# A cross-network kernel on one core: whole-tile transposes of the first input group, and the last round's outputs transposed on TensorE

## The chip, the cores and the metric

The kernel runs on 1 core of one Trainium2 chip. The metric is the device time of one execution in microseconds (us). Times are medians of several executions; a profile is one execution of its own. Executions are called fast or slow by their clock and time; only fast ones are compared. A ratio below is the mean time of one kernel's fast runs over the mean time of the other's fast runs of the same rounds, so it is not quite the ratio of the medians quoted beside it.

Engines are named as the profile names them: PE is TensorE, PEld its weight loads, DVE is VectorE, ACT is ScalarE, SP is SyncE. "SPq" and "ACTq" are DMA issues by SyncE and ScalarE: the time that the engine spends on handing a DMA over. A DMA lands when the last of its data have arrived.

## The reference

Six layers, each `x = x0 * (x @ w + b) + x`, on a batch of 16384 rows of 416 columns in bf16:

```python
B, F, D, L = 16384, 26, 16, 6        # Din = F * D = 416
def reference(x0, ws, bs):
    x = x0
    for l in range(ws.shape[0]):
        proj = jnp.einsum('bd,de->be', x, ws[l]) + bs[l]
        x = x0 * proj + x
    return x
```

## The kernel before

The batch is cut into 8 groups of 2048 rows (`GC`), each in 4 chunks of 512 (`CH`). The data are held transposed: features on the 128 partitions, rows along the free dimension. 416 features are three full tiles of 128 and a tail of 32. Two groups form a round, and PE alternates between them layer by layer, so that ScalarE (bias, out of PSUM, which the kernel's products are written to) and VectorE (multiply and add) can finish one group while PE works on the other. One group in one layer is called a job here; there are 48.

Group 0 is loaded by small transposing DMAs, 512 rows each. The 32-feature tail of groups 0 and 1 comes in a tile of its own, `Tbuf` (the last 128 features, of which 32 are used):

```python
            load_w(0, ("main",))                     # three DMAs of 104 KB
            for t in range(NMT):
                for j in range(G_CH):
                    load_x0_chunk_g0(t, j)           # 12 transposes of 512 x 128
            load_T(0)                                # Tbuf, 2048 x 128
            load_w(0, ("tail",))                     # four DMAs of 26 KB, one per copy
            ...
            load_group(1)                            # 3 transposes of 2048 x 128
            load_T(1)                                # waits until job 1 is done
```

The first two jobs do their full-row products, and then the 32-row products with `Tbuf`:

```python
                if tdirect:                          # layer 0 of groups 0 and 1
                    emit_full(g, l, 0, xin, nb_of, waits_tj)   # 12 products, waits per chunk
                    emit_full(g, l, 1, xin, nb_of, waits_tj)   # 12 products
                    pe.wait_ge(sem_T, 16 * pe_T_uses[0])
                    ...
                    emit_k32(g, l, 0, None, nb_of, True)       # 4 products of 32 rows
                    emit_k32(g, l, 1, None, nb_of, True)
                    ...                              # copy of the tail through PSUM, tile 2, tail
```

At the end a group has to be transposed back. Groups 0 to 6 are stored to a DRAM scratch, read back by a transposing DMA, and stored to the output; the last group, number 7, is transposed on PE, copied out of PSUM by ScalarE and VectorE and stored:

```python
            def out_group_dram(g):
                for i in range(NMT):
                    sp.wait_ge(sem_dve, eu_main_done(g, L - 1, i) + 1)
                    sp.dma_start(x6T[g, i * P:(i + 1) * P, :], xl[i][:, :]).then_inc(sem_scr, 16)
                ...                                  # the tail, in four DMAs
                sp.wait_ge(sem_scr, 16 * n_scr[0])
                for j in range(G_CH):
                    sp.dma_start_transpose(ost[os_][:, :, :], x6T[g, :, j * CH:(j + 1) * CH])...
                for j in range(G_CH):
                    sp.wait_ge(sem_otr[os_], 16 * n_otr[os_])
                    sp.dma_start(out[row0:row0 + CH, :]..., ost[os_][:, :, :])...
```

## Time and profile before

| | before |
|---|---|
| time, median of 6 runs | 537.33 us (535.80 to 538.16) |
| span of the profiled run | 535.4 us |
| PE busy | 94% |
| TensorE clock granted, mean | 0.984 |

First some lines of the page of the kernel before: the span; busy time of PE and its weight loads; the rows of busy tenths for PE and the DMA engines in 40 slices; HBM traffic; and the shares of the chain that ended last.

```profile
span 535.4 us, 7931 instructions
...
PE 504.7 (94%) x3168; PEld 192.9 (36%) x3168; DVE 375.5 (70%) x420; ACT 384.1 (72%) x640; POOL 0.7 (0%) x6
...
PE   2799999999999999999999999999999999999970
...
DMA  6768810000597990000497991000398900000179
...
HBM read 2.56 MB, written 25.56 MB: 53 GB/s over the span
...
PE 89%; SPq 3%; DVE 3%; DMA 2%; ACT 2%; issue 0%; ACTq 0%; DVEq 0%
```

PE is the bottleneck: 94% busy, 89% of the chain. The row of tenths shows where it is not: the first slices and the last.

To see how much of the run that touches, I cut every trace at two events: the start of the 32-column products of job 2, and the start of those of job 48. The three pieces are called start, middle and end:

| piece | before, us |
|---|---|
| start (to the 32-column products of job 2) | 45.58 |
| middle (46 jobs) | 468.47 |
| end (to the end of the span) | 21.34 |

The middle is 10.18 us per job, PE never idle. Anything to be won without making PE's work smaller lies in the start and the end.

Next, the chain of waits of the kernel before, at its start (start in us, length in us, what). L234 is the issue of the small transposes, L456 the full products, L474 the products with the 32-row tail.

```profile
2.13 1.21 SPq L234
...
15.12 1.26 SPq L234
...
16.42 2.83 DMA x0T<-in_x_dram
...
19.30 5.07 PE ps L456 x13
24.37 0.33 PE ps L474
...
32.05 5.59 DMA Tbuf<-in_x_dram
```

SyncE needs 1.26 us to issue each of the twelve transposes. The last lands at 19.25; PE then still has 13 products to do, at 0.39 us each (later 0.225 us), starts the products with Tbuf at 24.3 and can't start job 2 before 31.9.

The end of the kernel before, from its timeline (start, length, engine, line, operation). L280 is the transposing read of group 6, L499 the last product of the last job, L615 the last addition, L391 and L286 the output stores of groups 7 and 6.

```profile
514.22 8.33 SPq L280 DMA_TRANSPOSE ost<-x6T_scratch  x4
...
514.81 0.40 PE L499 MATMUL ps<-x,w 32*32 32x512 bf16 x4
...
518.91 0.42 DVE L615 TENSOR_TENSOR x<-tmps,x 128x512 bf16<-128x512 bf16 x1
...
521.54 0.42 ACTq L391 DMA_DIRECT2D out_dram<-tmpw  x1
...
522.60 5.07 SPq L286 DMA_DIRECT2D out_dram<-ost  x4
```

And the DMA engines at the end of the kernel before, from the windows (stretch in us; its length and busy us of PE, PEld, DVE, ACT and POOL; clock; mean share of the 16 DMA engines; GB/s):

```profile
525.00:530.00 5.00, 0.00 (x0) 0.00 (x0) 0.00 (x0) 0.00 (x0) 0.00 (x0) 0.50 1.11 338
530.00:534.00 4.00, 0.00 (x0) 0.00 (x0) 0.00 (x0) 0.00 (x0) 0.00 (x0) 0.50 1.11 331
```

From 525 to 534 nothing runs but DMA, at some 335 GB/s. Most of the eight output stores of 416 KB of groups 6 and 7 leaves in this stretch, and they begin late: the first is issued 6.3 us after PE's last product ended at 515.2, and group 6's wait for its transposes.

### The profile page before, as it was taken

How to read it: one execution, taken by the hardware profiler on the slowest of the kernel's cores; microseconds unless marked ns; L12 is line 12 of the kernel's file. 1: busy time of each engine (PE TensorE's matmuls, PEld its weight loads, DVE VectorE, ACT ScalarE, POOL GpSimd, SP SyncE). 2: the span in 40 equal slices, each digit the busy share in tenths (PEclk: the TensorE clock that was granted, in tenths of full speed). 3: DMA queues.
4: the chain of work that ended last, by engine and by line, in shares of the span. 5: the costliest groups of instructions: out<-in, count | busy, mean ns of one | idle time of the engine just before them, and what ended most of it. 6: DMA issues, size and time to landing. Idle time of an engine off the chain costs nothing.

```text
span 535.4 us, 7931 instructions
## 1 busy us (share of the span) xinstructions
PE 504.7 (94%) x3168; PEld 192.9 (36%) x3168; DVE 375.5 (70%) x420; ACT 384.1 (72%) x640; POOL 0.7 (0%) x6
## 2 busy tenths in 40 slices
PE   2799999999999999999999999999999999999970
PEld 0233333333333333333333333333333333333330
DVE  0056678678678778777777867867877877777790
ACT  1166777777887777777887777778787777777761
POOL 0000000000000000000000000000000000000000
PEclk9998999999999999999999999999999999999995
DMA  6768810000597990000497991000398900000179
GB/s 99 140 150 177 176 40 1 1 1 1 167 227 231 236 219 3 1 1 1 154 200 245 249 210 25 1 2 0 99 191 275 243 2 0 1 1 0 41 174 298
DMA packets 142565, 57.35 MB, mean 107 GB/s; under 512 B 119488, under 2 KB 139840, under 8 KB 142528
## 3 DMA queue, kind: packets, MB, share of 16 engines
q1 hardware_dynamic: 137232, 55.13, 44.1%
q10 hardware_dynamic: 5296, 1.71, 1.4%
q8 instruction: 25, 0.41, 0.3%
q14 instruction: 12, 0.10, 0.0%
HBM read 2.56 MB, written 25.56 MB: 53 GB/s over the span
## 4 chain that ended last, share of the span: by engine, by line
PE 89%; SPq 3%; DVE 3%; DMA 2%; ACT 2%; issue 0%; ACTq 0%; DVEq 0%
PE ps L456 70%; PE ps L474 9%; PE ps L482 7%; PE ps L499 3%; SPq L234 3%; ACT tmpw L377 1%; DVE x L615 1%; DMA Tbuf<-in_x_dram 1%; DVE tmpw L654 1%; DMA x0T<-in_x_dram 1%; PE ps L438 0%; SPq L222 0%; DVE tmpw L684 0%; DVE tmpw L649 0%; ACTq L391 0%
## 5 line engine op out<-in xcount | busy, mean ns | idle before, releaser
L377 ACT ACTIVATE tmpw<-ps,bias_f 128x512 bf16<-128x512 f32 x576 | 348.2, 688 | 128.3 <-PE ps L474 128.3
L456 PE MATMUL ps<-x,w 128*128 128x512 bf16 x1440 | 331.6, 380 | 0.0
L649 DVE TENSOR_TENSOR tmpw<-tmpw,x0T 128x2048 bf16<-128x2048 bf16 x141 | 172.8, 1225 | 146.7 <-ACT tmpw L377 146.6
L456 PEld LDWEIGHTS ps<-x,w 128*128 128x128 bf16 x1440 | 131.0, 98 | 169.5 <-issue 27.6
L615 DVE TENSOR_TENSOR x<-tmpw,x 128x2048 bf16<-128x2048 bf16 (+1 forms) x129 | 147.5, 1143 | 0.0
L456 PE MATMUL ps<-x0T,w 128*128 128x512 bf16 x288 | 74.5, 404 | 13.3 <-DMA x0T<-in_x_dram 12.7
L474 PE MATMUL ps<-x,w 32*128 32x512 bf16 x552 | 54.4, 385 | 0.0
L456 PEld LDWEIGHTS ps<-x0T,w 128*128 128x128 bf16 x288 | 27.3, 101 | 55.1 <-issue 16.2
L474 PEld LDWEIGHTS ps<-x,w 32*128 32x128 bf16 x552 | 13.9, 91 | 58.5 <-issue 58.5
L377 ACT ACTIVATE tmps<-ps,bias_f 128x512 bf16<-128x512 f32 x48 | 33.8, 705 | 0.0
L482 PE MATMUL ps<-x,w 128*32 128x512 bf16 x480 | 33.2, 383 | 0.0
L615 DVE TENSOR_TENSOR x<-tmpw,x0T 128x2048 bf16<-128x2048 bf16 x24 | 29.1, 1218 | 0.0
L660 DVE TENSOR_TENSOR tmps<-tmps,x 128x512 bf16<-128x512 bf16 x48 | 20.1, 418 | 0.0
L615 DVE TENSOR_TENSOR x<-tmps,x 128x512 bf16<-128x512 bf16 x48 | 20.1, 418 | 0.0
L499 PE MATMUL ps<-x,w 32*32 32x512 bf16 x184 | 18.2, 385 | 0.0
L482 PEld LDWEIGHTS ps<-x,w 128*32 128x32 bf16 x480 | 9.1, 95 | 13.4 <-issue 9.1
L499 PEld LDWEIGHTS ps<-x,w 32*32 32x32 bf16 x184 | 4.5, 87 | 19.5 <-issue 19.5
L482 PE MATMUL ps<-x0T,w 128*32 128x512 bf16 x96 | 6.7, 383 | 0.0
L474 PE MATMUL ps<-Tbuf,w 32*128 32x512 bf16 x24 | 5.9, 376 | 0.4 <-DMA Tbuf<-in_x_dram 0.4
L355 ACT ACT_TABLE_LOAD x1 | 1.3, 1283 | 5.4 <-issue 5.4
L379 ACT ACTIVATE tmps<-ps 128x512 bf16<-128x512 f32 x8 | 5.0, 628 | 0.0
L654 DVE TENSOR_TENSOR tmpw<-tmpw,x0T 128x512 bf16<-128x512 bf16 x12 | 4.9, 416 | 0.0
(26 smaller groups left out, 25.3 us busy)
## 6 DMA issues: line engine op xcount, KB each, us to landing
out_dram<-ost SPq DMA_DIRECT2D x28, 416.0 KB, 5.4
x6T_scratch<-x SPq DMA_DIRECT2D x21, 512.0 KB, 3.8
w<-in_ws_dram SPq DMA_DIRECT2D x18, 104.0 KB, 2.4
out_dram<-tmpw ACTq DMA_DIRECT2D x3, 416.0 KB, 5.7
x6T_scratch<-x SPq DMA_DIRECT2D x28, 32.0 KB, 2.4
w<-in_ws_dram SPq DMA_DIRECT2D x24, 26.0 KB, 1.8
x0T<-in_x_dram SPq DMA_TRANSPOSE x33, 4.6
ost<-x6T_scratch SPq DMA_TRANSPOSE x28, 4.6
```

The lines of the kernel that those rows point to most:

```text
L234: sp.dma_start_transpose(x0T[s][t][:, j * CH:(j + 1) * CH], x0[j * CH:(j + 1) * CH, t * P:(t + 1) * P]).then_inc(sem_g0[t][j], 16)
L355: act.activation(bias_f[:, :, :], bias_bf[:, :, :], ACT_F.Copy).then_inc(sem_act, 1)
L377: act.activation(dst, src, ACT_F.Identity, bias=bias_ap, scale=1.0).then_inc(sem_act, 1)
L379: act.activation(dst, src, ACT_F.Copy).then_inc(sem_act, 1)
L456: pe.matmul(bank_ap(nb_of[(i, j)]), wm[l][t][:, ecols], xin[t][:, j * CH:(j + 1) * CH], start=(t == 0), stop=False,)
L474: pe.matmul(bank_ap(nb_of[(i, j)]), lhsT, rhs, start=False, stop=True, tile_position=tp).then_inc(sem_pe, 1)
L482: pe.matmul(bank_ap(n, j * TAIL, (j + 1) * TAIL), wm[l][t][:, ecols], xin[t][:, j * CH:(j + 1) * CH], start=(t == 0), stop=False, tile_pos ...
L499: ins = pe.matmul(bank_ap(n, j * TAIL, (j + 1) * TAIL), lhsT, rhs, start=False, stop=True, tile_position=tp)
L615: dve.tensor_tensor(o_ap, t_ap, i_ap, ALU.add).then_inc(sem_dve, 1)
L649: dve.tensor_tensor(tw[:, :], tw[:, :], x0T[s][i][:, :], ALU.mult).then_inc(sem_dm, 1)
L654: dve.tensor_tensor(tw[:, cols], tw[:, cols], x0T[s][i][:, cols], ALU.mult).then_inc(sem_dm, 1)
L660: dve.tensor_tensor(tw[:, 0:CH], tw[:, 0:CH], x03[s][:, :], ALU.mult).then_inc(sem_dm, 1)
```

## The change

It is meant to shorten both ends. At the start: whole tiles of group 0 are loaded by three transposes instead of twelve; PE takes the first job's products in the order in which the input tiles arrive; the four copies of the weight tail come by one DMA with a broadcast source; the bias comes by one DMA of plain rows and is turned by seven tiny products on PE; and 24 dummy products are meant to warm PE up. At the end: group 6, too, is transposed on PE, after job 48, and then group 7.

```diff
+    N_WARM = 24
...
+    pe_groups = [g for g in range((NR - 1) * R, NG) if g != GFIN] + [GFIN]     # groups 6, 7
+    fin_tiles = [(g, j, k) for g in pe_groups for j in range(G_CH) for k in range(KT)]
...
+            pair_eng += ["a", "a", "d", "a", "a", "d", "a", "d"][:NPG]         # group 6: ScalarE or VectorE copies
+            pair_eng += ["d", "d", "d", "d", "a", "d", "d", "d"][:NPG]         # group 7
...
-                    for j in range(Q):
-                        sp.dma_start(w3[l][j * TAIL:(j + 1) * TAIL, :], ws[l, NMT * P:D, :]).then_inc(sem_w[l], 16)
+                    src = ws[l, NMT * P:D, :].unsqueeze(0).broadcast_to([Q, TAIL, D])
+                    sp.dma_start(w3[l][:, :], src).then_inc(sem_w[l], 16)
...
             load_w(0, ("main",))
             for t in range(NMT):
-                for j in range(G_CH):
-                    load_x0_chunk_g0(t, j)
+                load_x0_tile_g0(t)
             load_T(0)
-            load_w(0, ("tail",))
...
+            act.dma_start(bias_rows[0:L, :], bs[:, :]).then_inc(sem_bias, 16)
+            act_load_w(0, ("tail",))
...
+            for _w in range(N_WARM):
+                pe.matmul(psum[:, (NBANK - 1) * CH:(NBANK - 1) * CH + P], ident[:, :], ident[:, :], ...)
...
-                    emit_full(g, l, 0, xin, nb_of, waits_tj)
-                    emit_full(g, l, 1, xin, nb_of, waits_tj)
+                    if g == 0:
+                        emit_full_pair((0, 1), xin, nb_of, waits_tj)           # by input tile
+                    else:
+                        emit_full(g, l, 0, xin, nb_of, waits_tj)
+                        emit_full(g, l, 1, xin, nb_of, waits_tj)
...
+            for gi, g in enumerate(pe_groups):
+                ...
+                pe.wait_ge(sem_dve, eu_last(g, L - 1) + 1)
+                for b0 in range(base, base + NPG, BLK):                        # blocks of 4 pairs
+                    ...                                                        # transposes, then tails
```

The tail of a group in DRAM scratch is also stored by one DMA instead of four.

## The prediction

> **What bounds the kernel now.** The page gives a span of 535.4 us (537.3 timed); the chain that ended last is 89% PE. In the timeline's middle a job (one group, one layer) takes about 10.15 us with PE never idle: 48 jobs, about 487 us, untouched by the change. About 48 us lie outside, at the two ends.
>
> *Start.* The chain of waits begins with SyncE issuing twelve 512-row x0 transposes, 1.26 us each. The last lands at 19.25; then PE needs 5.07 us for 13 matmuls (0.39 us each, later 0.225), starts the products with Tbuf at 24.30 and job 2 at 31.94. Full 2048-row transposes, later in the trace, issue in 2.26 us and land 4.4 to 5.0 us after their issue begins.
>
> *End.* PE ends its last product at 515.2, VectorE its last add at 519.3. The first output store of the last group issues at 521.54, those of group 6 (stored to DRAM and transposed back until 524) from 522.6. The windows show DMA saturated (330 GB/s) until 534.0: eight stores of 416 KB, nearly 10 us; the span ends 1.3 us later.
>
> **What changes.**
> 1. Start: three transposes replace twelve, issued at 2.13, 4.4, 6.7 us, Tbuf at 9.0; landings about 7, 9.4, 11.6, 13.7 (estimate from the durations above). PE does eight matmuls per tile, 3.4 us while cold. The Tbuf products start near 14.7 (13.7 to 16) against 24.30. The rest of job 1 (7.6 us) is unchanged: gain 9.6 us (8.3 to 10.6), all on the critical path.
> 2. Warm-up: 24 matmuls of 128 columns in idle PE time. [...]I give it little. The trace agrees that sparse matmuls stay slow (0.61 us each until 19 us).
> 3. Bias by one DMA and seven small matmuls: off the path; its 3184 tiny packets leave the DMA engines.
> 4. Merged tail loads and stores: [...]PE waits for none. About 0.
> 5. End: group 6's 64 transposes (61 ns each in the timeline) fit PE's idle 515.2 to 519.3. ScalarE is free at 517.15 and copies pairs 0 and 1 (four copies of 0.47 us), so the first store issues near 519.1, with no DMA transposes before it. [...] DMA works 520.6 to 530.4, the end comes near 531.7: gain 3.5 us (2 to 4.5). Group 7's last copies stay near 525 and don't starve the DMA.
>
> **Sum.** 537.3 − 9.6 − 3.5 = **524.2 us, range 521.5 to 527.8**. Faster by over 2% (below 526.6): 0.83; within 2%: 0.16; slower: 0.01.
>
> **What would show it.** Timeline: Tbuf products at 14 to 16, job 2 at about 22; middle still 10.15 us per job; first output store about 4 us after PE's last job product (now 6.3); DMA saturated for about 10 us before the end.
>
> **What would make it wrong.** First full tiles landing well after 5 us (the start then gains 7 to 8); PE cold through all 24 matmuls; group 7's transposes or copies held behind group 6's, so the last stores leave late; stores slower than 330 GB/s.

The sum reads 537.3 − 9.6 − 3.5 = 524.2 us. The warm-up and the merged loads count for nothing in it; in the end's 3.5 us, the 1.5 us between the first store's issue (519.1) and the start of the DMA's work (520.6) is an assumption that no trace here shows (0.9 us was measured).

## The result, and the profile after

| | before | after |
|---|---|---|
| time, median | 537.26 us (16 runs, 535.14 to 538.85) | 523.43 us (8 runs, 522.00 to 524.42) |
| ratio of fast runs | | 0.9745 (95%: 0.9731 to 0.9760) |
| span of the profiled run | 535.4 us | 521.6 us |
| start | 45.58 us | 35.84 us |
| middle | 468.47 us | 468.47 us |
| end | 21.34 us | 17.31 us |

The change is faster by 2.55%. The middle is the same to a hundredth of a microsecond; 9.74 us came from the start and 4.03 us from the end. The page after:

```profile
span 521.6 us, 8079 instructions
...
PE 505.3 (97%) x3263; PEld 198.2 (38%) x3263; DVE 378.2 (73%) x430; ACT 386.3 (74%) x646; POOL 0.7 (0%) x6
...
PE   5999999999999999999999999999999999999992
...
DMA  9799300000797990000597990000379900000008
...
HBM read 2.56 MB, written 23.86 MB: 51 GB/s over the span
...
PE 91%; DVE 3%; SPq 2%; ACT 1%; DMA 1%; issue 0%; DVEq 0%; ACTq 0%
```

HBM writes fell by 1.70 MB: group 6's detour. The chain of waits after, at its start (L241 is the issue of a whole-tile transpose, L528 the products with the tail, L494 the full products):

```profile
2.13 4.16 SPq L241
...
6.34 2.12 SPq L241
...
8.50 2.18 SPq L241
...
10.72 5.66 DMA Tbuf<-in_x_dram
...
16.42 0.40 PE ps L528
...
24.13 5.29 PE ps L494 x24
```

Three issues and the load of Tbuf now stand where twelve issues stood. The products with Tbuf start at 16.42 instead of 24.3, job 2 at 24.1 instead of 31.9. Note the first issue: 4.16 us, where the prediction took 2.26.

The end after, from the timeline. L553 is the last product of the last job, L632 the transposes, L427 ScalarE's copies of group 6, L341 the stores of group 6.

```profile
505.07 0.40 PE L553 MATMUL ps<-x,w 32*32 32x512 bf16 x4
...
505.40 1.51 PE L632 MATMUL ps<-ident,x 128*128 128x128 bf16 x24
...
507.27 3.39 ACT L427 ACTIVATE x<-ps 128x416 bf16<-128x416 bf16 x8
...
509.06 2.14 SPq L341 DMA_DIRECT2D out_dram<-x  x3
```

The transposes of group 6 follow the last job without a gap; the first store is issued at 509.06, 3.6 us after PE's last job product ended at 505.47 (6.3 before). The windows at the end:

```profile
509.00:510.00 1.00, 0.36 (x4) 0.23 (x4) 1.00 (x4) 1.00 (x4) 0.00 (x0) 1.00 0.02 7
510.00:512.00 2.00, 1.83 (x36) 1.66 (x36) 1.60 (x7) 1.47 (x4) 0.00 (x0) 1.00 1.02 321
512.00:520.00 8.00, 1.35 (x29) 1.15 (x26) 3.70 (x14) 0.93 (x2) 0.00 (x0) 0.81 1.02 326
520.00:521.60 1.60, 0.00 (x0) 0.00 (x0) 0.00 (x0) 0.00 (x0) 0.00 (x0) 0.50 0.30 97
```

DMA is saturated from 510 to 520.5, at 321 to 326 GB/s. The end is still bound by the same eight stores, but they begin earlier, and no transposing DMA stands before them.

### A part of the start's gain that no line of the diff shows

Job 1 gave 7.88 us (16.42 against 24.30, with the rest of the job equal). The remaining 1.87 us of the 9.74 came from job 2, which nobody had meant to change. A part of it is a wait. Before, PE reached job 2's products with Tbuf 0.40 us ahead of the data; after, the data were there. From the PE timelines, before:

```profile
37.69 1.90 PE L474 MATMUL ps<-Tbuf,w 32*128 32x512 bf16 x8 [0.40 <-DMA Tbuf<-in_x_dram]
```

and after:

```profile
29.35 1.89 PE L528 MATMUL ps<-Tbuf,w 32*128 32x512 bf16 x8
```

From the start of job 2 to these products it is 5.75 us before (31.94 to 37.69) and 5.28 after (24.07 to 29.35), which makes 0.47 us. The other 1.40 us come after them, and the windows show why. First before, at two neighbouring stretches of 3.41 us in job 2 (the column before the DMA share is the clock):

```profile
37.22:40.63 3.41, 2.87 (x16) 1.00 (x15) 0.06 (x1) 2.52 (x5) 0.00 (x0) 1.00 0.44 107
40.63:44.04 3.41, 3.41 (x8) 1.09 (x9) 2.32 (x3) 2.70 (x5) 0.00 (x0) 0.50 0.58 127
```

Then after, at the same place in job 2:

```profile
28.83:32.24 3.41, 3.28 (x17) 1.05 (x15) 0.01 (x1) 2.47 (x5) 0.00 (x0) 1.00 0.56 138
32.24:35.66 3.42, 3.22 (x14) 1.19 (x14) 2.33 (x2) 3.11 (x6) 0.00 (x0) 1.00 1.08 198
```

The entries of the clock record of these two traces last 3.413 us or a multiple of it (before: 17.067, 3.413 and 477.866 us; after: 3.413, 3.413 and 505.173 us), all but the last, with which the record ends. Before, a stretch at half clock (0.50) fell into job 2, from 40.63 to 44.04 us; after, none did. Within each stretch I counted, from the trace's records, the columns that PE streamed, weighted by the share of the 128 rows in use. In the first 40 us of all profiles with a clock record, at full clock, stretches that had work in them and counted 2560 or fewer were all followed by half clock (five, in five profiles; one is the 2048 of the run with the tail later, one the 2432 of the longer warm-up, both below); of six with 3072, four were; with 3584 or more, none was. The low stretches are those of the Tbuf products, which use 32 of the 128 rows: PE was busy 2.87 of 3.41 us in the first line above, and the clock still fell. These are counts of the profiles here, not a rule. If they decide, which no run isolates, then it depends on where the stretches happen to begin whether a run pays a half-clock stretch in job 1, in job 2, or in neither.

### The profile page after: what moved, and what is told of

It reads as the page before. It is cut to its first block, busy times and chain, and to the rows that moved or that the text cites. A ratio compares the mean times of both kernels' runs of the same rounds, so it can differ in the third digit from the quotient of the medians.

```text
span 521.6 us, 8079 instructions
## 1 busy us (share of the span) xinstructions
PE 505.3 (97%) x3263; PEld 198.2 (38%) x3263; DVE 378.2 (73%) x430; ACT 386.3 (74%) x646; POOL 0.7 (0%) x6
## 4 chain that ended last, share of the span: by engine, by line
PE 91%; DVE 3%; SPq 2%; ACT 1%; DMA 1%; issue 0%; DVEq 0%; ACTq 0%
PE ps L494 72%; PE ps L528 9%; PE ps L536 7%; PE ps L553 3%; SPq L241 2%; ACT tmpw L398 1%; DVE x L680 1%; DMA Tbuf<-in_x_dram 1%; DVE tmpw L719 1%; DVE x L749 1%; PE ps L476 0%; PE ps L632 0%; SPq L229 0%; DVE tmpw L714 0%; DVE tmpw L749 0%
## 5 line engine op out<-in xcount | busy, mean ns | idle before, releaser
L494 PE MATMUL ps<-x,w 128*128 128x512 bf16 x1440 | 331.6, 380 | 0.0
L494 PEld LDWEIGHTS ps<-x,w 128*128 128x128 bf16 x1440 | 131.0, 98 | 169.5 <-issue 27.6
L494 PE MATMUL ps<-x0T,w 128*128 128x512 bf16 x264 | 61.3, 380 | 0.7 <-ACT tmpw L398 0.6
L528 PE MATMUL ps<-x,w 32*128 32x512 bf16 x552 | 54.4, 385 | 0.0
L494 PEld LDWEIGHTS ps<-x0T,w 128*128 128x128 bf16 x264 | 24.1, 98 | 33.0 <-issue 5.4
L528 PEld LDWEIGHTS ps<-x,w 32*128 32x128 bf16 x552 | 13.9, 91 | 58.5 <-issue 58.5
L553 PE MATMUL ps<-x,w 32*32 32x512 bf16 x184 | 18.2, 385 | 0.0
L553 PEld LDWEIGHTS ps<-x,w 32*32 32x32 bf16 x184 | 4.5, 87 | 19.5 <-issue 19.5
L510 PE MATMUL ps<-x0T,w 128*128 128x512 bf16 x24 | 7.0, 455 | 4.5 <-DMA x0T<-in_x_dram 4.5
L632 PE MATMUL ps<-ident,x 128*128 128x128 bf16 x96 | 6.3, 220 | 1.0 <-DVE x L680 0.8
L427 ACT ACTIVATE x<-ps 128x416 bf16<-128x416 bf16 x10 | 4.3, 565 | 3.3 <-DVE x L749 3.3
L528 PE MATMUL ps<-Tbuf,w 32*128 32x512 bf16 x24 | 5.9, 376 | 0.3 <-DMA Tbuf<-in_x_dram 0.3
```

Of the source, the lines that this page charges most:

```text
L494: pe.matmul(bank_ap(nb_of[(i, j)]), wm[l][t][:, ecols], xin[t][:, j * CH:(j + 1) * CH], start=(t == 0), stop=False,)
L510: pe.matmul(bank_ap(nb_of[(i, j)]), wm[0][t][:, i * P:(i + 1) * P], xin[t][:, j * CH:(j + 1) * CH], start=(t == 0), stop=False,)
L528: pe.matmul(bank_ap(nb_of[(i, j)]), lhsT, rhs, start=False, stop=True, tile_position=tp).then_inc(sem_pe, 1)
L553: ins = pe.matmul(bank_ap(n, j * TAIL, (j + 1) * TAIL), lhsT, rhs, start=False, stop=True, tile_position=tp)
L632: pe.transpose(pt[:, r0 + i * P:r0 + (i + 1) * P], xl[i][:, cols], ident[:, :])
```

## The experiments

All edits are to the changed kernel unless it is said otherwise. "Start" and "end" are the pieces defined above. Every kernel gave a correct result. Only the three experiments run beside the first repetition (the transposes taken back, the old order, the products spread out) can be compared with the changed kernel in the same rounds; the others are compared by their ratios to the kernel before, which ran beside all of them.

### The same two kernels again

No edit. First the changed kernel:

> The changed kernel unaltered, as the yardstick for its neighbours on this chip and for a second look at its start. If the start varies from execution to execution by the phase of the clock record (half-clock windows of 3.41 us that follow a window with little full-row work), its profile may show the Tbuf products of the first job anywhere from 14.9 to 16.5 us and one half-clock window or none in jobs 1 and 2; the ratio to before should be 0.973 to 0.977.

Measured: 523.26 us, ratio 0.9743 (0.9717 to 0.9769); start 34.89, middle 468.47, end 17.32. The end repeats to 0.01 us; the start is 0.95 us shorter than in the first profile. Its PE timeline:

```profile
7.87 7.67 PE L510 MATMUL ps<-x0T,w 128*128 128x512 bf16 x24 [3.33 <-DMA x0T<-in_x_dram]
15.47 1.90 PE L528 MATMUL ps<-Tbuf,w 32*128 32x512 bf16 x8
```

Here PE ran all 24 products without a wait, at about 0.32 us each on average, and the tail products followed at once: PE's own pace (0.32 us a product, 0.225 us later), not the landing, set this start. In the first profile it was the landing of Tbuf. The two are about a microsecond apart, and either may come last.

Then the kernel before:

> The kernel before, unaltered, for a second look at its start. In its first profile the last chunk landed at 19.25 us, the Tbuf products began at 24.30, and a half-clock window (40.63 to 44.04) fell into job 2, whose length was 14.8 us. If that window comes and goes by phase, job 2 may be about 13.1 us here and the third job begin near 45; if the clock dip always belongs to this order, job 2 is again near 14.8 us. The Tbuf products should begin within 0.7 us of 24.3.

Measured (one run): 537.36 us, start 45.92, middle 468.47, end 21.18. The Tbuf products began at 24.70, and there was again one half-clock stretch, this time in job 1 (27.84 to 31.26); the time between the 32-column products of jobs 1 and 2 was 13.19 us instead of 14.73. So a stretch at half clock is paid in both profiles of before, in one job or the other: here job 1 took 8.03 us from its Tbuf products to its 32-column products, against 6.56 in the second profile of the changed kernel, and job 2 kept a wait for Tbuf (0.33 us longer than the 12.86 of the changed kernel). It was expected to come and go, and it did move.

### The whole-tile transposes taken back

```diff
-                load_x0_tile_g0(t)
+                for j in range(G_CH):
+                    load_x0_chunk_g0(t, j)      # one semaphore per chunk, as before
```

> The changed kernel with the twelve 512-row transposes of before in place of the three full ones; everything else as changed. Theory A (the issue time of the transposes is what the start gained): the last chunk issues near 16.4, Tbuf lands near 21.9, the Tbuf products start near 22 against 16.42, the time is 5 to 6.5 us above the changed kernel, about 529. Rival (the bias packets slowed the chunks, and without them chunks issue well under 1.26 us): the loss is under 3 us.

Measured: 532.48 us, ratio 0.9907 (0.9878 to 0.9937), against 0.9743 for the changed kernel in the same rounds: 9.2 us lost by the medians. Start 44.60, end 17.30. From its PE timeline (L531 is the products with Tbuf; the bracket tells PE's idle time before them and what ended it):

```profile
22.71 2.30 PE L531 MATMUL ps<-Tbuf,w 32*128 32x512 bf16 x8 [2.07 <-DMA Tbuf<-in_x_dram]
```

The twelve issues took 15.64 us, as before, though the bias packets are gone: the rival falls. Tbuf lands at 22.7, PE waits 2.07 us for it with little to do, and two half-clock stretches follow (24.07 to 30.90). From its Tbuf products to its 32-column products job 1 then took 9.03 us against 6.56, 2.5 us that were not expected; the Tbuf products themselves came 6.3 to 7.2 us later than in the two profiles of the changed kernel. Of the start's 9.7 to 11.0 us (both pairs of profiles), this one edit is 8.8 to 9.7; all other edits at the start together make the difference between 44.60 and 45.58 or 45.92, about 1 us.

### Group 6 sent through DRAM again

```diff
-    pe_groups = [g for g in range((NR - 1) * R, NG) if g != GFIN] + [GFIN]
+    pe_groups = [GFIN]
```

> The changed kernel with group 6 sent again through DRAM scratch and transposing DMA (only the last group transposed on PE). Theory A (the end gives about 4 us: stores begin 2 to 3 us earlier after PE's last product and nothing transposes in front of them): slower than the changed kernel by 3.5 to 5 us, 527 to 528.5, and still about 9 to 10 us faster than before. Rival (the end's gain comes from something else, as the new assignment of the copies or the merged tail stores): slower by less than 1.5 us.

Measured: 528.40 us, ratio 0.9857 (0.9840 to 0.9873). Start 35.71, end 22.16, which is 4.85 us more than with the change. From its timeline (L284 transposes of group 6, L632 PE's transposes of group 7, L290 stores of group 6):

```profile
505.95 6.90 SPq L284 DMA_TRANSPOSE ost<-x6T_scratch  x4
...
509.51 2.74 PE L632 MATMUL ps<-ident,x 128*128 128x128 bf16 x24 [4.18 <-DVE x L680]
...
512.91 3.49 SPq L290 DMA_DIRECT2D out_dram<-ost  x4
```

PE idled 4.18 us before group 7's transposes, the first store was issued at 512.91, 7.6 us after PE's last job product (ended at 505.34) instead of 3.6, and four transposing DMAs stood before it. The theory holds. The loss exceeds the 4.03 us between before and after, probably (no run tests it) because the changed kernel's order for group 7 alone is worse than that of before, which transposed two of the three tiles while VectorE was still working on the third: the end is 22.16 against 21.34.

### Without the warm-up

```diff
-    N_WARM = 24
+    N_WARM = 0
```

> The changed kernel without its 24 warm-up matmuls. The clock record shows that they raised the clock to full only from about 4.9 to 8.3 us, and that it was half again from 8.3 to 11.75, when the first tile's products ran. Theory A (the warm-up does nothing here, the transposes bound the start): time within 0.6 us of 523.4, Tbuf products between 16.4 and 17.2. Rival (the warm-up is part of the gain): slower by 1.5 us or more, Tbuf products after 17.8.

Measured: 523.08 us, ratio 0.9760 (0.9743 to 0.9776); start 35.83, Tbuf products at 16.41. The intervals overlap those of the changed kernel (0.9745 and 0.9743); nothing is seen to be lost, though a loss of up to some 2 us would lie within them. In the changed kernel's first profile the clock record begins after the warm-up with full clock, from 4.94 to 8.35 us, but the first tile landed at 8.56, and the clock was half until 11.76.

### A longer warm-up

```diff
             ins.then_inc(sem_bp, 1)
+            for _w in range(40):
+                pe.matmul(psum[:, (NBANK - 2) * CH:(NBANK - 2) * CH + P], ident[:, :], ident[:, :],
+                          start=True, stop=True)
```

> The changed kernel with 40 more 128-column warm-up matmuls after the bias products, so that PE stays busy until about 7 us, when the first tile lands. Theory D (the first tile's 16 to 24 products at half clock now bound the start, as in the second profile of the changed kernel, where PE ran them for 7.67 us without a wait): clock full from the first tile on, the products follow the landings, Tbuf products start at 14.2 to 15.2 (15.5 to 16.4 before this edit), 0.5 to 1.5 us faster. Rival (only the landings count): the same within 0.4 us.

Measured: 526.56 us, ratio 0.9804 (0.9778 to 0.9831): slower than the changed kernel, against both theories. Start 38.36, end 18.45. Its PE timeline (L513 full products, L531 Tbuf products):

```profile
8.01 1.67 PE L513 MATMUL ps<-x0T,w 128*128 128x512 bf16 x7
10.95 3.82 PE L513 MATMUL ps<-x0T,w 128*128 128x512 bf16 x16 [1.27 <-DMA x0T<-in_x_dram]
16.41 3.05 PE L531 MATMUL ps<-Tbuf,w 32*128 32x512 bf16 x8 [1.64 <-DMA Tbuf<-in_x_dram]
```

The clock was full from 6.76 us, as wanted, and the products ran at about 0.24 us each. PE was done with them at 14.77, waited 1.64 us for Tbuf, and the 32-row products came next: 2432 weighted columns in that stretch, then two at half clock (17.00 to 23.82).

This does not refute theory D, because something else moved as well. Tbuf landed 6.68 us after its issue, against 4.81 us in the second profile of the changed kernel. And the page counts 26 instruction loads of 16 KB in queue 8, where that of the changed kernel, without the 40 products, counts 25; the second line here is a window at the end:

```profile
q8 instruction: 26, 0.43, 0.3%
...
523.00:524.00 1.00, 0.00 (x0) 0.00 (x0) 0.00 (x0) 0.00 (x0) 0.00 (x0) 0.50 0.09 27
```

The trace's DMA packets have one of these loads at 13.95 to 15.46 us, while Tbuf was on its way, and from 15 to 16 us DMA moved only 12 GB/s. Another lies at 514.01 to 515.13, among the stores; in the profiles with 25 loads the last one began before the first store was issued. After 523.1 us what was still in flight were rows of the last stores, 832 bytes each, one after another until 524.21: 26 packets in the last microsecond of the stores, against 334 to 371 in the fast profiles with 25 loads. That explains the longer end as far as the packets show it. That the instruction loads are the cause is not tested by a run of its own; the run with three edits below, which has the same 40 products, shows both signs again. So it stays open what a full clock at the start would give if nothing else moved. What is shown is that these 40 products cost some 3 us, and that PE, once faster, waited for Tbuf.

### The weight tail in four DMAs, or later

```diff
-            act_load_w(0, ("tail",))
+            for j in range(Q):
+                act.dma_start(w3[0][j * TAIL:(j + 1) * TAIL, :], ws[0, NMT * P:D, :]).then_inc(sem_w[0], 16)
```

> The changed kernel, but the first layer's 32-row weight tail loaded again as four DMAs (one per copy, still issued from ScalarE) instead of one broadcast DMA whose outermost dimension is 4. In the changed kernel the first full transpose took 4.16 us to issue[...]. Theory A[...]: the first transpose issues in 2.2 to 2.6 us, the Tbuf products start near 14.6 instead of 16.42, the time falls by 1.5 to 2.0 us to about 521.7. Theory B (it is the first transpose behind the three weight loads, whatever the tail does): issue stays near 4.1 us, Tbuf products at 16.2 to 16.6, time within 0.5 us of 523.4.

Theory A, here and in the next run, is that the tail load in front holds up the first transpose.

Measured: 522.71 us (median of the four fast runs), ratio 0.9756 (0.9736 to 0.9776), the same as the changed kernel within the intervals. Its profiled execution was slow (1273 us, PE steps of 0.62 us for 512 columns most of the time; in the profile of before a step is 0.427 us at half clock and 0.216 us at full clock), so its times inside are not compared. Its first transpose issue took 2.61 us.

```diff
-            act_load_w(0, ("tail",))
...
             load_T(0)
+            load_w(0, ("tail",))
```

> The changed kernel, but the same single broadcast tail load is issued by SyncE after the first Tbuf transpose, so nothing but the three weight loads stands before the transposes. Theory A[...]: first transpose issues in about 2.3 us, Tbuf lands near 14, and the products with it start at 14.3 to 15 (the tail load, issued near 11.2, should land by then); time about 521.5 to 522. Theory B (weight loads or a cold start of the queue): as the changed kernel, 523.4 within 0.5, perhaps slower because the tail comes later.

Measured: 524.39 us, ratio 0.9791 (0.9769 to 0.9812); slower than the changed kernel. The first transpose issued in 2.27 us and the products of the first tile began at 6.94, but the tail, now last, held the Tbuf products up until 16.00: PE waited 1.78 us for it, the stretch counted 2048, and half clock followed (18.30 to 21.71). Start 36.46.

Of theory A the first half stands: with the one broadcast DMA in front, the first issue of a whole tile took 2.77 to 4.16 us in eight profiles; without it in front, 2.27 in one profile (and 2.44 and 2.61 in the two with four DMAs, the second of them slow). Why the load should hold the transpose up is not shown: the trace as I read it does not tell the DMA engines apart. And theory A's gain of 1.5 to 2 us did not come. In the late version the tail itself was late; of the four DMAs alone there is no profile in the fast state that shows where the gain went.

### The old order of the first job's products

```diff
-                    if g == 0:
-                        emit_full_pair((0, 1), xin, nb_of, waits_tj)
-                    else:
-                        ...
+                    emit_full(g, l, 0, xin, nb_of, waits_tj)
+                    emit_full(g, l, 1, xin, nb_of, waits_tj)
```

> The changed kernel with the first job's products in the old order (all of output tile 0, then all of tile 1) instead of by input tile. The third input tile lands near 14.1, and 16 products (3.6 us) then follow instead of 8: the Tbuf products start near 17.8 instead of 16.42, time 0.8 to 1.8 us above the changed kernel. If the transposes' arrival alone counted, it would be within 0.4 us.

Measured: 524.51 us, ratio 0.9773 (0.9741 to 0.9805), against 0.9743 (0.9717 to 0.9769): unclear. Its profile shows no loss: Tbuf products at 15.37, start 34.78. Here the first transpose was issued in 2.85 us, not 4.16, so the last tile landed at 11.76 instead of 14.15, and the 16 products after it took 3.63 us, as expected. The expected delay was reckoned from a landing that did not repeat; this one profile does not tell what the order of the products is worth.

### The Tbuf products spread out

```diff
-                    emit_k32(g, l, 0, None, nb_of, True)
-                    emit_k32(g, l, 1, None, nb_of, True)
+                    for j in range(G_CH):
+                        k32d(0, j)                       # a 32-row product of tile 0
+                        full1(NMT - 1, 1, j)             # a full-row product of tile 1, held back until here
+                    for j in range(G_CH):
+                        k32d(1, j)
```

> The changed kernel with the last four full-row products of output tile 1 put between the four 32-row Tbuf products of tile 0, in jobs 1 and 2. The clock records so far have a half-clock window right after a window with only 2048 to 3072 full-row columns, which is the stretch of the Tbuf products. Theory C (such a stretch, falling in one window by its phase, halves the clock for 3.41 us and costs up to 1.7 us): no half-clock window in jobs 1 and 2, and 0.5 to 1.5 us faster than the changed kernel on average, with less spread. Rival (these windows don't matter for the time, or come from something else): the same within 0.4 us.

Measured: 523.96 us, ratio 0.9755 (0.9728 to 0.9782): no gain. In the profile no stretch at full clock counted under 4096 and no half-clock stretch followed, as theory C said; but start was 35.69, within the 34.89 to 35.84 of the changed kernel, whose two profiles had no half-clock stretch there to save. Each product took 0.32 us instead of 0.225 while 32-row and full-row products alternated, and job 2 took 13.02 us instead of 12.86. Two of its four executions had a mean clock of 0.988 and two of 0.994, with times of 524.48 and 524.30 against 523.62 and 523.25; if the lower ones are a half-clock stretch at the start, the edit did not prevent all of them. That is not settled.

### The first output chunk in two halves

```diff
+                    if c == 0:
+                        for h in range(2):
+                            sp.wait_ge(sem_cpa, cum_a[gi * NPG + h])
+                            r0 = row0 + h * 2 * P
+                            sp.dma_start(out[r0:r0 + 2 * P, :]..., stg[:, 2 * h:2 * h + 2, :]).then_inc(sem_fin2, 16)
```

> The changed kernel with the first output chunk of group 6 stored as two halves, each as soon as its pair of tiles is copied out. Theory E (the end is the time of the first store plus some 10.5 us of saturated DMA plus 1.1 us): the first store issues about 0.9 us earlier after PE's last job product (2.8 instead of 3.7 us), the saturated stretch begins as much earlier, and the end comes 0.7 to 0.9 us earlier. Rival (the last copies of group 7 or the last store's landing set the end): unchanged within 0.3 us in the profile's end section.

Measured: 522.87 us, ratio 0.9736 (0.9712 to 0.9759), not distinguishable from the changed kernel. In the profile the first store came 0.82 us earlier within the end (3.93 us after its beginning instead of 4.75), but the end was 17.06 us, only 0.25 shorter. The windows show where the rest went:

```profile
509.00:510.00 1.00, 0.24 (x9) 0.14 (x8) 1.00 (x4) 1.00 (x4) 0.00 (x0) 1.00 0.44 152
510.00:511.00 1.00, 0.79 (x11) 0.62 (x12) 1.00 (x4) 1.00 (x4) 0.00 (x0) 1.00 0.80 257
511.00:512.00 1.00, 1.00 (x25) 0.90 (x21) 0.67 (x3) 0.87 (x3) 0.00 (x0) 1.00 0.49 163
```

DMA started earlier, and then fell back between 510 and 512: the second chunk holds a pair that VectorE copies, and VectorE was still at the last additions and began that copy at 509.90. Theory E was half right: the first store sets the end only as long as the second follows in time.

### Three edits together

The four-DMA tail, the 40 extra dummies and the halves, all in one:

> The changed kernel with three edits together: first weight tail as four DMAs, 40 more warm-up matmuls, first output chunk in halves. If each does what its theory says: Tbuf products at 13.8 to 14.6, end section 0.8 us shorter, about 521 (ratio to before 0.969 to 0.972). If only the end edit works: about 522.5.

Measured: 526.15 us, ratio 0.9802 (0.9774 to 0.9831): slower than the changed kernel, like the longer warm-up alone. Start 35.75 with a half-clock stretch (17.70 to 21.11) after a wait of 1.41 us for Tbuf; end 19.02. The signs of the longer warm-up are here again: 26 instruction loads, one at 13.13 to 14.21 us while Tbuf was on its way (it landed 5.73 us after its issue), one at 511.23 to 512.89 among the stores, and only 26 packets of the stores in their last microsecond. No version tried is shown to beat the changed kernel.

## Why the prediction was right

- **Total.** Predicted 524.2 us (521.5 to 527.8), measured 523.43. The division was predicted as 9.6 us at the start and 3.5 at the end; the profiles show 9.74 and 4.03.
- **The middle.** It was said to be untouched; it is 468.47 us in both, and in every variant that ran at a normal clock.
- **The start.** The mechanism (twelve issues of 1.26 us stood on the path) is shown by the experiment that takes the whole-tile transposes back: 9.2 us, of which 2.5 us are half clock that followed. But that the size was right was luck, by errors that cancel. "The Tbuf products start near 14.7": they started at 16.42 in the first profile (just outside the 14 to 16 that was offered as a test) and at 15.47 in the second. The terms mis-sized there were the first issue (2.26 us assumed, 3.2 to 4.2 measured, with the tail DMA in front) and, in the first profile, Tbuf's landing (4.7 us assumed, 5.66 measured). "The rest of job 1 is unchanged" holds in the first pair. The Tbuf products thus gained 7.88 us in the first pair and 9.23 in the second. What was added, and the prediction had not reckoned with, was the half-clock stretch after the Tbuf products that both profiles of before pay and these two profiles of the changed kernel do not (1.40 us in the first pair, 1.47 in the second) and a shorter wait in job 2 (0.47 and 0.33). In the second pair the start gained 11.03 us in all, more than the 8.3 to 10.6 that was offered.
- **The warm-up.** "I give it little" was right: removing it costs nothing that was measured. The reason given was not shown. In the first profile the clock record has full clock after the burst, from 4.94 us on, and half clock again 0.2 us before the first tile landed (8.35 against 8.56).
- **The merged loads.** "About 0" is right for the time. That "PE waits for none" was too simple: with the merged tail load in front the first transpose took 0.5 to 1.9 us longer to issue (2.77 to 4.16 against 2.27), and PE does wait for the first tile. Moving or splitting the load gained nothing that was measured.
- **The bias.** It was not tested alone. Together with the rest of the small edits at the start it is bounded by about 1 us.
- **The end.** The chain was as predicted: group 6's transposes in PE's idle time, first store about 4 us after PE's last job product (3.6 measured), saturated DMA of about 10 us (10.5), nothing starved. The gain was 4.03 us instead of 3.5: the first data moved 0.9 us after the first issue, where the prediction allowed 1.5 (519.1 to 520.6), and the stores took 10.6 us from first to last packet, where it took 9.8 (520.6 to 530.4), so here too two misses nearly cancel; sending group 6 back through DRAM loses 4.85 us of the end.

## What to carry to other kernels

Cut the trace into the steady part and the two ends before costing a change; here the steady part did not move by 0.01 us, and the whole result was readable at the ends. At a start like this one count DMA issues, not only bytes: for the same bytes, twelve issues of a quarter tile took about twice the time of three whole ones (15.55 against 8.55 us). Where PE was faster at the start, as with the longer warm-up, it then waited for Tbuf (1.64 us), and after the stretch with that wait and the 32-row products the clock was half for 6.8 us (17.00 to 23.82). So a fix of one arrival is worth no more than the next arrival allows: measure where the next wait sits before making it. The 40 added products came with one instruction load more (26 against 25), and the page lists these loads among the DMA queues: compare their number and place before the edit itself is blamed.
